# Last head transposes, feed-forward input sums and the last down product, reordered in a fused attention and feed-forward kernel

## The chip, the cores and the metric

The kernel runs on one core of one Trainium2 chip. The metric is the device time of one execution, in microseconds (us). Before the change it was 1168.09 us, the median of three runs (1167.99 to 1169.35). PE is the tensor engine (matmuls), PEld its weight loads, DVE the vector engine, ACT the scalar engine, POOL GpSimd, SP the sync engine. SP and ACT issue the DMA transfers. In the traces, DMA queue q1 carries what SP issues and q10 what ACT issues. L267 is line 267 of the kernel in question. Line numbers shift by a few between versions, so L905 of before is L909 of after, and L977 is L974 in one experiment.

## The reference

Cut to what matters: one transformer block, adaptive layernorm, 32 query heads over 512 keys, then a gated feed-forward network.

```python
# x: (1, 2048, 1024); 32 query heads, 4 key/value heads of 128; F = 3584; all bf16
sa, ca, ga, sb, cb, gb = six rows of silu(c) @ w_mod
h = layernorm(x) * (1 + ca) + sa
q = h @ wq                        # per head 128 columns
p = softmax(q @ k.T * 128**-0.5)  # the last 512 keys of the cache
x = x + ga * (concat_heads(p @ v) @ wo)
h = layernorm(x) * (1 + cb) + sb
x = x + gb * ((silu(h @ w_gate) * (h @ w_up)) @ w_down)
```

## The kernel before

The 2048 rows go through attention in four chunks of 512, 32 heads each. Then comes the chunk's output projection `oproj`. Then two feed-forward stages of 1024 rows each follow, each ending in a "down" product. The large products run as seven smaller ones over sums and differences of blocks (A11, A12, S1, S2, ... on the input side, and the same for the weights), numbered 0 to 6 below. The S sums are made by the vector engine. Weights arrive in "units" of 512 KB, issued by ACT into a few slots.

A head's output is transposed by a DMA on the sync queue, one head late, and four layernorm transposes (`ln_turn`) are issued at head 29, ahead of the last heads:

```python
def oturn(i):
    h = hd(i)
    T.op(tr_queue(), lambda: SP.dma_start_transpose(oT[:, h, :]..., o_sb[i % NOS]),
         reads=[B_os[i % NOS]], writes=B_oT[h])
# in the loop over heads; i counts all heads of all chunks
if ch == NCH - 1 and h == 29:
    ...
    for a_ in kept:
        ln_turn(*a_)
...
pv(i, ...)                      # p @ v of head i, and its division on the vector engine
if i >= 1:
    oturn(i - 1)
```

The output projection goes through its seven products. Between matmuls it calls `each()`, which takes one task from a list that belongs to the coming feed-forward stage. Product 0 loads the chunk's rows of x at its end:

```python
for n in range(len(PRO)):                       # the seven products
    both = n < 4
    for part in range(1 if both else 2):
        for ws in ((0, 1), (2, 3)):             # units of four head pairs
            for k in (0, 1) if both else (part,):
                for w_ in ws:
                    for p in range(NPU * w_, NPU * w_ + NPU):
                        o_mm(n, k, p)
                    each()
            ...
            if n or ws[0]:
                while free:
                    u = free.pop(0)
                    if u < UPC:                 # product 0: behind the last head's transpose
                        load_unit(ch, u, 1, B_oT[hd(Hq - 1)] if n == 0 else ())
            if n == 0 and ws[0]:
                for t in range(TPC):
                    load_x(ch * TPC + t)
        ...
    if n == 0:
        sums(2)                                 # the S2 sums, for product 2
```

The task list is one queue: eight layernorm scalings, then eight "stretch sums", then loads and pair sums at fixed positions. `load_raw` loads gate and up weights:

```python
todo = [lambda kc=kc: ln_scale(1, kc, ...) for kc in range(DT)] + stretch_todo()
rest = [lambda m=m, k=k: sums_of_pair(0, m, k) for m in range(2) for k in range(4)]
at = {18: lambda: load_raw(0), 24: ..., 28: lambda: load_raw(1), 46: lambda: load_raw(2)}
at.update((36 + j, f_) for j, f_ in enumerate(rest))
```

At the end of the kernel each 128x512 tile of the last down product is evicted by `take_product`: add the sum kept in `u_`, multiply by the gate, add to the rows. Then the 256 KB of whole rows are stored.

```python
V.tensor_tensor(u_[0], bank(b), u_[0], ALU.add)
V.tensor_tensor(rt[s_], u_[0], gate[:, lo:lo + CH], ALU.mult)
V.tensor_tensor(x_[:, lo:lo + CH], x_[:, lo:lo + CH], rt[s_], ALU.add)
```

The softmax here doesn't subtract the row's maximum and nothing guards it: scores larger than these inputs give would overflow.

## Time and profile before

| | before |
|---|---|
| median, range | 1168.09 us (1167.99 to 1169.35), 3 runs |
| span of the profiled run | 1165.9 us, clock 1.0 |
| PE, DVE, ACT busy | 98%, 67%, 45% |
| last output projection | about 605.9 to 653.8 us |
| end of the last matmul (its start, 1161.28, plus 0.216), end of the last vector work, last store landed | 1161.5, 1163.57, 1165.61 us |

The lines themselves are in the prediction below. PE is busy nearly all the time, so read the profile for the few places where PE waits and for the tail after its last matmul.

One warning on the column of idle time. The profile models the end of a matmul, 0.38 us after its start, while such matmuls follow one another every 0.216 us. A wait of 1.0 us therefore shows as only about 0.8. In this trace 118 matmul records are missing as well: it has 7789, and the trace of e4 below, a kernel with the same matmuls, has 7907. A missing record leaves 2 x 0.216 - 0.38 = 0.05 us of seeming idle time, so as an estimate some 6 of the 13.4 us of PE's idle time were never idle. Below, a "loss" is counted from start to start: the distance between two matmul starts, less what the first takes at full rate.

### The profile page before, as it was taken

What the parts mean: (1) busy time and instruction counts of PE and PEld (TensorE: products, weight loads), DVE (VectorE), ACT (ScalarE), POOL (GpSimd) and SP (SyncE); (2) the same over time, 40 slices, a digit from 0 to 9 for tenths busy, and PEclk for the clock granted to TensorE, in tenths of its full rate; (3) what the DMA queues carried; (4) which work ended last, traced back from release to release, by engine and by line L of the source; (5) the groups of instructions that cost most, each with busy time, mean ns of one, the idle gap of its engine ahead of it and who ended that gap; (6) DMA issues with size and microseconds to landing.
All of it is one profiled execution on the core that took longest, in us unless ns stands there. A gap on an engine that the chain in (4) does not pass through costs nothing.

```text
span 1165.9 us, 20810 instructions
## 1 busy us (share of the span) xinstructions
PE 1146.7 (98%) x7789; PEld 669.7 (57%) x7907; DVE 786.7 (67%) x1718; ACT 526.2 (45%) x844; POOL 21.7 (2%) x41
## 2 busy tenths in 40 slices
PE   8999999999999999999999999999999999999998
PEld 5787645777548876468864444444444444444443
DVE  4888646877638877347847688888377777776214
ACT  3777503777217775057751244444110344444110
POOL 1000000000000000000000000000010000000000
PEclk9999999999999999999999999999999999999999
DMA  9999796999859997869949765666895232322733
GB/s 289 246 250 260 203 357 231 262 272 257 268 202 284 272 218 210 306 149 287 272 99 349 247 176 182 206 180 175 276 246 179 86 86 77 105 73 65 261 126 135
DMA packets 283876, 245.57 MB, mean 211 GB/s; under 512 B 109952, under 2 KB 247168, under 8 KB 283776
## 3 DMA queue, kind: packets, MB, share of 16 engines
q1 hardware_dynamic: 253328, 179.74, 58.3%
q10 hardware_dynamic: 30448, 64.50, 15.6%
q8 instruction: 63, 1.03, 0.4%
q14 instruction: 37, 0.30, 0.1%
HBM read 189.27 MB, written 30.41 MB: 188 GB/s over the span
## 4 chain that ended last, share of the span: by engine, by line
PE 95%; DMA 2%; DVE 1%; ACT 1%; issue 1%; POOL 0%; DVEq 0%; ACTq 0%
PE ps L267 95%; DMA arena<-in_A_wo_dram 1%; ACT arena L758 1%; DMA arena<-arena 0%; PE ps L271 0%; DVE arena L775 0%; ACT arena L1025 0%; DMA arena<-in_c_dram 0%; ACT arena L742 0%; DVE arena L977 0%; DVE arena L492 0%; DVE arena L372 0%; DVE arena L707 0%; DVE arena L774 0%; DVE arena L980 0%
## 5 line engine op out<-in xcount | busy, mean ns | idle before, releaser
L267 PE MATMUL ps<-arena 128*128 128x512 bf16 (+5 forms) x7740 | 1144.3, 308 | 13.4 <-DVE arena L500 1.2
L267 PEld LDWEIGHTS ps<-arena 128*128 128x128 bf16 (+1 forms) x7858 | 666.9, 98 | 488.4 <-issue 6.8
L758 ACT ACTIVATE arena<-ps 128x1024 bf16<-128x1024 f32 x256 | 262.0, 1027 | 37.6 <-PE ps L267 34.8
L644 DVE TENSOR_TENSOR arena<-arena 128x512 f16<-128x512 bf16 (+3 forms) x510 | 223.1, 481 | 26.5 <-DMA wo_sums<-arena 13.5
L703 ACT ACTIVATE arena<-ps 128x256 f32<-128x256 f32 x180 | 68.7, 382 | 136.7 <-PE ps L267 136.2
L1304 DVE TENSOR_TENSOR arena<-ps,arena 128x512 f16<-128x512 f32 x112 | 77.3, 690 | 40.0 <-PE ps L267 37.9
L1297 ACT ACTIVATE arena<-ps 128x512 f32<-128x512 f32 x112 | 66.9, 597 | 73.6 <-PE ps L267 73.6
L707 DVE TENSOR_TENSOR arena<-ps,arena 128x256 bf16<-128x256 f32 x180 | 75.8, 421 | 32.6 <-PE ps L267 30.4
L775 DVE TENSOR_TENSOR arena<-ps,arena 128x512 bf16<-128x512 f32 x128 | 88.5, 692 | 4.5
L1326 ACT ACTIVATE ps<-ps 128x512 f32<-128x512 f32 x56 | 32.6, 582 | 119.7 <-PE ps L267 119.4
L977 DVE TENSOR_TENSOR arena<-ps,arena 128x512 f32<-128x512 f32 x34 | 23.4, 689 | 87.7 <-PE ps L267 87.6
L774 DVE RECIPROCAL arena<-ps 128x4 f32<-128x4 f32 x128 | 23.2, 181 | 52.5 <-PE ps L267 52.4
L1316 DVE TENSOR_TENSOR arena<-ps,arena 128x512 bf16<-128x512 f32 x56 | 38.6, 688 | 29.7 <-ACT arena L1311 29.7
L1311 ACT ACTIVATE arena<-ps 128x512 f16<-128x512 f32 x56 | 33.3, 595 | 31.6 <-PE ps L267 31.6
L980 DVE TENSOR_TENSOR arena<-ps,arena 128x512 bf16<-128x512 f32 x22 | 15.2, 689 | 46.0 <-PE ps L267 46.0
L428 DVE BATCH_NORM_STATS2 arena<-arena 128x6 f32<-128x512 bf16 x56 | 38.4, 687 | 9.1 <-DMA arena<-x_mid 8.8
L1008 DVE SCALAR_TENSOR_TENSOR arena<-arena 128x512 f32<-128x512 bf16 x56 | 41.6, 743 | 0.1
L1311 ACT ACTIVATE arena<-arena 128x512 f16<-128x512 f16 x56 | 34.8, 622 | 4.9 <-DVE arena L1304 4.9
L379 POOL TENSOR_TENSOR arena<-arena 128x1 f32<-128x1 f32 x30 | 19.2, 641 | 849.1 <-DVE arena L377 849.1
L929 ACT ACTIVATE arena<-ps 128x512 f32<-128x512 f32 x12 | 6.8, 596 | 60.8 <-PE ps L267 60.8
L905 DVE TENSOR_TENSOR arena<-arena 128x1024 f16<-128x1024 bf16 (+1 forms) x48 | 29.7, 686 | 6.2 <-DMA arena<-arena 6.2
L1316 DVE TENSOR_TENSOR arena<-arena 128x512 bf16<-128x512 f16 x56 | 23.8, 425 | 5.0
(61 smaller groups left out, 200.7 us busy)
## 6 DMA issues: line engine op xcount, KB each, us to landing
arena<-wo_sums ACTq DMA_DIRECT2D x46, 512.0 KB, 8.7
arena<-in_A_wq_dram SPq DMA_DIRECT2D x42, 512.0 KB, 4.9
arena<-wq_sums SPq DMA_DIRECT2D x22, 768.0 KB, 6.7
arena<-in_B_w_gate_dram SPq DMA_DIRECT2D x28, 512.0 KB, 4.2
arena<-in_B_w_up_dram SPq DMA_DIRECT2D x28, 512.0 KB, 5.4
arena<-wd_sums ACTq DMA_DIRECT2D x16, 896.0 KB, 6.6
arena<-in_A_wo_dram SPq DMA_DIRECT2D x24, 512.0 KB, 6.5
arena<-in_B_w_down_dram ACTq DMA_DIRECT2D x12, 896.0 KB, 7.4
```

The lines of the kernel that those rows point to most:

```text
L267: T.op(PE, lambda: TE.matmul(out_ap, lhsT, rhs, start=start, stop=stop, skip_group_check=loose), reads=reads, writes=bb)
L428: T.op(DVE, lambda: V.bn_stats(st_sb[i][:, 6 * hf:6 * hf + 6], x_[:, 512 * hf:512 * hf + 512]), reads=[bx], writes=[B_st[i]])
L644: T.op(st, lambda: e.tensor_tensor(dst, x, y, op), reads=reads, writes=[dst_b])
L703: T.op(ACT, lambda: A.activation(sn[k], bank(QBK, 256), AF.Copy), writes=PB[QBK] + [B_sn[k]])
L707: T.op(DVE, lambda: V.tensor_tensor(dst, bank(XBK, 256, off), sn[k], ALU.add), reads=[B_sn[k]], writes=PB[XBK] + [B_q[i % NQ]])
L758: T.op(ACT, lambda: A.activation(ex[i % NEX][:, kt:kt + 2, :], bank(SCB[kt], 1024).rearrange("p (a b) -> p a b", a=2), AF.Exp, scale=att_s ...
L775: T.op(DVE, lambda: V.tensor_tensor(o_sb[i % NOS].rearrange("p (a b) -> p a b", a=TPC), num, rl_bc, ALU.mult), reads=[B_rl], writes=both + ...
L1008: T.op(DVE, lambda: V.scalar_tensor_tensor(acc, ms[:, kc, :], sc[:, kc:kc + 1], acc, op0=ALU.mult, op1=ALU.add), reads=[B_ms, B_sc, B_acc] ...
L1297: T.op(ACT, lambda: A.activation(fn[m][i], bank(b), AF.Copy), writes=PB[b] + [B_fn[m][i]])
L1304: T.op(DVE, lambda: V.tensor_tensor(ring[c_], bank(b), fn[m][i], ALU.add), reads=[B_fn[m][i]], writes=PB[b] + [bs[c_]])
L1311: T.op(ACT, lambda: A.activation(sl_[c_], src, AF.Silu), reads=reads, writes=writes + [B_sl[c_]])
L1316: T.op(DVE, lambda: V.tensor_tensor(dst, u_[0], s_[0], ALU.mult), reads=[s_[1]] + [x for x in u_[1:]], writes=[db] + list(bb))
```

## The change

Its intent is to take away PE's waits in the last output projection, and to shorten the vector work and the store behind the last matmul. It has four parts.

```diff
 # 1. the last four heads are transposed at once; product 0 takes both tiles pair by pair
+            def turned(i):
+                return i >= NA - 4
...
-                        for ws in ((0, 1), (2, 3)):
-                            for k in (0, 1) if both else (part,):
+                        for ws in ((0, 1), (2, 3)) if n else ((0, 1), (2,), (3,)):
+                            if n == 0 and ws[0]:
+                                for p in range(NPU * ws[0], NPU * ws[-1] + NPU):
+                                    o_mm(n, 0, p)
+                                    o_mm(n, 1, p)
+                            for k in ((0, 1) if both else (part,)) if n or not ws[0] else ():
...
-                if i >= 1:
+                if i >= 1 and not turned(i - 1):
                     oturn(i - 1)
+                if turned(i):
+                    oturn(i)
 # 2. the tasks are bound to a product
+            first = {1: [... ln_scale ...],
+                     2: [None] * 5 + [lambda: load_raw(0), ...],
+                     3: stretch_todo(), 4: rest, 5: [None] * 6 + [lambda: load_raw(2)]}
+            first[4].insert(2, lambda: load_raw(1))
 # 3. the rows of x are loaded at head 26 instead of after product 0
-                            if n == 0 and ws[0]:
-                                for t in range(TPC):
-                                    load_x(ch * TPC + t)
+                if ch and h == Hq - 6:
+                    for t in range(TPC):
+                        load_x(ch * TPC + t)
 # 4. the last down product: rows prepared ahead, two operations a tile, last tile in halves
+                        for k in range(4):
+                            ... u2[k] = u2[k] * gate;  u2[k] = u2[k] + x_
+                        ... the same for the part already in bank cb[3], second half
+                        for k in range(4):
+                            ... store the second half of the rows now
+                            for lo, w in ((0, CH),) if k < 3 else ((0, half_), (half_, half_)):
+                                ... matmuls, then u1 = bank * gate; x_ = u1 + u2
+                                ... store these columns on a queue of their own
```

More of the change, by code (lines that the diff above doesn't have):

```diff
@@ L947, in oproj @@
                                         o_mm(n, k, p)
-                                    each()
+                                    each(n)
                             if both or part:
                                 free.extend(n * PPU + w_ + NUN for w_ in ws)
-                            if n or ws[0]:
+                            if n or ws[0] == 3:
                                 while free:
@@ L1211, in _ @@
                 if h == Hq - 1:
-                    oturn(i)
+                    if not turned(i):
+                        oturn(i)
                     if ch == 0:
@@ L1224, in _ @@
                     else:
-                        oproj(ch, (), lambda: None)
+                        oproj(ch, (), lambda n: None)
             NST, NPR, TPS = 2, FT // 2, 2 * TPC
@@ L1387, in stretch_todo, with each @@
                 return [lambda k=k, j=j: stretch_sums(k, j) for k in range(4) for j in range(2)]
-            todo = [lambda kc=kc: ln_scale(1, kc, g2, B_g2, sb, B_sb) for kc in range(DT)] + stretch_todo()
             rest = [lambda m=m, k=k: sums_of_pair(0, m, k) for m in range(2) for k in range(4)]
-            at = {18: lambda: load_raw(0),
-                  24: lambda: T.op(ACT, lambda: A.activation(shift, shift, AF.Silu), reads=B_shift, writes=B_shift),
-                  28: lambda: load_raw(1), 46: lambda: load_raw(2)}
-            at.update((36 + j, f_) for j, f_ in enumerate(rest))
-            todo += [at.pop(j, lambda: None) for j in range(len(todo), 47)]
-            def each():
-                if todo:
-                    todo.pop(0)()
+            todo = []
+            first = {1: [lambda kc=kc: ln_scale(1, kc, g2, B_g2, sb, B_sb) for kc in range(DT)],
+                     2: [None] * 5 + [lambda: load_raw(0),
+                         lambda: T.op(ACT, lambda: A.activation(shift, shift, AF.Silu), reads=B_shift, writes=B_shift)],
+                     3: stretch_todo(), 4: rest, 5: [None] * 6 + [lambda: load_raw(2)]}
+            first[4].insert(2, lambda: load_raw(1))
+            def each(n):
+                for _ in range(1 + (len(first.get(n, ())) > 8)):
+                    if first.get(n):
+                        f_ = first[n].pop(0)
+                        if f_:
+                            f_()
             oproj(NCH - 1, o_done, each)
-            while todo:
-                todo.pop(0)()
+            assert not any(first.values())
             def take_small():
@@ L1494, in _ @@
             Q_xr = [dq("q_xr%d" % i) for i in range(4)]
+            Q_end = [dq("q_end%d" % i) for i in range(5)]
             xr = {}
@@ L1503, in down @@
                 u2 = [None] * 4
+                last = st == NST - 1
                 for k in range(4):
@@ L1519, in down @@
                     w_ = n % NWD
+                    if last and n == len(PROD) - 1:
+                        for k in range(4):
+                            x_, bx = xr[4 + k]
+                            T.op(DVE, lambda: V.tensor_tensor(u2[k], u2[k], gb_bc[:, 0:CH], ALU.mult), reads=[B_gb[0]], writes=[B_u2[k]])
+                            T.op(DVE, lambda: V.tensor_tensor(u2[k], u2[k], x_[:, 0:CH], ALU.add), reads=[bx], writes=[B_u2[k]])
+                        half_ = CH // 2
+                        T.op(DVE, lambda: V.tensor_tensor(u1[3][:, half_:], bank(cb[3], half_, half_), gb_bc[:, half_:CH], ALU.mult),
+                             reads=[B_gb[0]], writes=PB[cb[3]] + [B_u1[3]])
+                        T.op(DVE, lambda: V.tensor_tensor(u2[3][:, half_:], u2[3][:, half_:], u1[3][:, half_:], ALU.add),
+                             reads=[B_u1[3]], writes=[B_u2[3]])
+                        for k in range(4):
+                            t = t0 + 4 + k
+                            x_, bx = xr[4 + k]
+                            B_xe = [_Buf("xe%d" % i) for i in range(2)]
+                            for b_ in B_xe:
+                                b_.absorb(bx)
+                            T.op(Q_out[k], lambda: SP.dma_start(of[t * P:(t + 1) * P, CH:D], x_[:, CH:D]), reads=[bx])
+                            for lo, w in ((0, CH),) if k < 3 else ((0, half_), (half_, half_)):
+                                b = ab[0] if lo else cb[k]
+                                for p in range(NPR):
+                                    mm(bank(b, w, lo), pt[a_][:, p, k * P:(k + 1) * P], wd[n % NWD][:, p, lo:lo + w], lo > 0 and p == 0, p == NPR - 1,
+                                       [B_pt[a_][p], B_wd[n % NWD][p // 7]], PB[b], loose=True)
+                                T.op(DVE, lambda: V.tensor_tensor(u1[k][:, lo:lo + w], bank(b, w, lo), gb_bc[:, lo:lo + w], ALU.mult),
+                                     reads=[B_gb[0]], writes=PB[b] + [B_u1[k]])
+                                T.op(DVE, lambda: V.tensor_tensor(x_[:, lo:lo + w], u1[k][:, lo:lo + w], u2[k][:, lo:lo + w], ALU.add),
+                                     reads=[B_u1[k], B_u2[k]], writes=[B_xe[lo > 0]])
+                                T.op(Q_end[k + (lo > 0)], lambda: SP.dma_start(of[t * P:(t + 1) * P, lo:lo + w], x_[:, lo:lo + w]),
+                                     reads=[B_xe[lo > 0]])
+                        continue
@@ L1566, in _ @@
                 order = [order[i] for i in (6, 7, 2, 3, 0, 4, 1, 5)]
-            for q_ in Q_out:
+            for q_ in Q_out + Q_end:
                 T.wait_all(q_)
```

## The prediction

> **What bounds the kernel now.** I read the page first, then the tensor engine's waits in the stretch the change edits, then the chain of waits there, the DMA view of the same stretch, and the timeline of the last microseconds. The page (line, engine, tiles, count, busy time and mean, idle time before and its releaser):
>
> ```profile
> span 1165.9 us, 20810 instructions
> PE 1146.7 (98%) x7789; PEld 669.7 (57%) x7907; DVE 786.7 (67%) x1718; ACT 526.2 (45%) x844; POOL 21.7 (2%) x41
> PE 95%; DMA 2%; DVE 1%; ACT 1%; issue 1%; POOL 0%; DVEq 0%; ACTq 0%
> L267 PE MATMUL ps<-arena 128*128 128x512 bf16 (+5 forms) x7740 | 1144.3, 308 | 13.4 <-DVE arena L500 1.2
> ```
>
> The tensor engine (PE) is the bound, at full clock, and the change takes no matmul away. It can only win back PE's idle time, 13.4 us in all, or shorten the tail after the last matmul. The change edits two places: the output projection of the last chunk (from 605.9 us to about 653.8 us) and the last down product. PE's waits between 604 and 660 us:
>
> ```profile
> PE ps L267 <- DMA arena<-arena: 1.1, 2, 0.9
> PE ps L267 <- DVE arena L977: 0.8, 1, 0.8
> PE ps L267 <- DMA arena<-in_A_wo_dram: 0.3, 1, 0.3
> PE ps L267 <- DVE arena L775: 0.2, 1, 0.2
> ```
>
> The first is a DMA transpose of a head's output, the second a PSUM eviction behind other vector work, the third a weight unit of the output projection. These figures count idle time after a modelled 0.38 us end of each matmul; start to start a 512-wide matmul takes 0.216 us, so the real losses are larger. Start to start I find: 0.33 and 1.07 us for two transposes (607.2, 607.7), 0.17 us for an input sum (617.7), 0.93 and 0.05 us for the eviction (624.8, 627.4), 0.41 us for the weight unit (642.2). Sum **2.97 us**. The 0.39 us at 604.6 is not touched.
>
> The chain of waits there (start, duration, what) shows that the last of them is more than its 0.3 us:
>
> ```profile
> 625.69 3.70 PE ps L267 x16
> ...
> 629.47 12.97 DMA arena<-in_A_wo_dram
> 642.44 0.14 issue
> 642.58 11.38 PE ps L267 x52
> ```
>
> That unit is issued when its slot is free, and lands 12.97 us later, because its queue is full. So PE and the DMA queue run neck and neck here.
>
> The tail, vector engine's timeline (start, duration):
>
> ```profile
> 1161.70 0.69 DVE L977 TENSOR_TENSOR arena<-ps,arena 128x512 f32<-128x512 f32 x1 [1.14 <-PE ps L267]
> 1162.42 0.69 DVE L980 TENSOR_TENSOR arena<-arena 128x512 bf16<-128x512 f32 x1
> 1163.15 0.42 DVE L981 TENSOR_TENSOR arena<-arena 128x512 bf16<-128x512 bf16 x1
> ```
>
> PE ends at 1161.7, three dependent operations end at 1163.57, and the store (2.0 us from issue to landing, in the issues list) ends the span.
>
> **What the Trainium skill says.** "DMA: Bandwidth & Descriptors", section "Queues, rings and completion order": each DMA engine round-robins between the queue rows that have work, a packet at a time. The trace agrees to the packet. From 622 to 630 us, and from 632 to 640 us (queue, packets, MB, share):
>
> ```profile
> q10 hardware_dynamic: 750, 2.73, 87.1%
> q1 hardware_dynamic: 750, 0.38, 16.8%
> ```
> ```profile
> q10 hardware_dynamic: 1735, 1.74, 70.4%
> q1 hardware_dynamic: 1736, 0.88, 41.4%
> ```
>
> One packet of q1 (the gate and up weights) passes for each one of q10 (the units), and the engines' time is used up. "VectorE: DVE Perf Modes", section "The TRN2 errata": a matmul costs 6+FD cycles at 2.4 GHz, so 216 ns for 512 columns and 109 for 256; the trace has 216 ns, and halving a tile costs PE nothing but 14 x 2 ns. The same section: an fp32 tensor_tensor takes (N+151)/0.96 ns, 691 for 512 and 424 for 256; the trace has 689, and 421 for its 256-wide PSUM additions. "DMA: Bandwidth & Descriptors", section "Anatomy of one DMA": about 2 us of a DMA are fixed, so quartering the last store saves little; the trace's 2.0 us for 256 KB agrees.
>
> **Part 1, heads turned at once, product 0 in another order.** Before, the sync queue issues four layernorm transposes (599.56 to 604.93), then the four last heads at 605.02, 606.34, 607.64 and 608.95, landing 2.4 us later each. Product 0 stands still for the first two (607.48, 608.76). After, only head NA-4 overtakes the layernorm transposes; its output is ready at 599.58. The count of transposes ahead of head NA-3 stays five in all, so it still lands at about 608.8. But the new order does both tiles of heads pair by pair: 12 matmuls from 605.89 need no new head, two more need NA-4, so the first that needs NA-3 comes at 605.89 + 14 x 0.216 = 608.91, just after 608.8. Gain 0.33 + 1.07, with 0.1 us in hand. Product 0 then ends near 609.3.
>
> **Part 2, sums held back.** Before, eight layernorm scalings (8 x 0.33 = 2.6 us) stood ahead of the S2 sums (four of 0.69 us), and eight stretch sums (5.5 us) ahead of product 1's eviction at 624.95. After, S2 begins at 614.5, when the S3 sums end, and its first tile is ready at 615.2, before product 2 at 616.3; then the scalings until 619.8, then the evictions at 619.8 and 621.6, before product 3 at 623.2. The stretch sums come in product 3, which has no eviction on the vector engine, and the pair sums in product 4, on which nothing waits until the feed-forward stage. Gain 0.17 + 0.93 + 0.05. Sum of parts 1 and 2: 2.56 us, with which PE asks for the last unit of product 5 near 639.6 instead of 642.2.
>
> **Part 3, x loaded six heads early: the unit queue decides.** The units can't start before the last head's turn lands (611.38, unchanged). They are 14 loads to the one PE waits for, ten of 128 packets of 4 KB and four of 512 packets of 1 KB, and the DMA engines are 90 to 100% busy. Taking the rows of x (1 MB) out helps only by what they took from the units. Between 613 and 621 us q1 sent 489 packets in 23.6% of 8 us, 1.9 us, most of them x. The gate weights, small packets, will follow at once, since nothing on the sync queue holds them: 489 x (16.8% of 8 us / 750) = 0.9 us. So about 1.0 us is saved, and some 0.2 us more since the gate weights start 2 us earlier, at 610.3, and send part of their packets before the units run. The last unit lands at about 642.4 - 1.2 = 641.2 and not at 639.6. Hence I expect PE to gain **1.2 us** of the 2.97 us in this stage (used at 641.35 against 642.58); the rest becomes a longer wait for the same unit. Moving x in the two middle chunks gains nothing: no DMA wait stands there.
>
> **Part 4, the last down product.** Added ahead of it on the vector engine: four times a product and a sum (0.725 + 0.61 us start to start, from the 0.69 us rows) and two halves of 0.42: 6.1 us from 1150.8 to 1156.9. Before, the first tile was evicted at 1152.63, so it starts 4.3 us behind, but a tile now costs two operations, 1.34 us, against PE's 3.02: tiles end at 1158.3, 1159.6, 1161.0, the first half of the last at 1161.8, where the second half becomes ready. The bank of tile 3 is read by 1156.9, before PE needs it at 1158.7. After the last matmul: 0.42 + 0.03 + 0.42 = 0.87 against 1.87 us, so 1.0 us; the store shrinks from 256 to 64 KB, I take 0.2 us. **1.2 us.**
>
> **Sum:** 1168.09 - 1.2 - 1.2 = **1165.7 us**.
>
> **Rivals.** (a) The units keep pace: all 2.97 us come home, 1163.9 us. For it: x is out of the way, and the 1 KB packets would go faster if the gate and up weights ran out. Against it: those are 4096 packets (2 MB), and one-for-one sharing uses them up only near the last unit. (b) The gate weights simply take x's place: no gain at all in this stage, 1166.9 us. For it: the first units landed only after 7 us even though x was half done by 614. Against: small packets take a third of the time. (c) The vector engine falls behind in the last product, or tile 3's bank is late: plus up to 1 us at the end. Against it: 1.8 us in hand at the bank. (d) Head NA-3's transpose is late: 0.1 to 0.5 us lost again, but under part 3 this vanishes behind the unit anyway.
>
> **Range and chances.** I give the unit queue 60%, (a) 20%, (b) 20%; the tail is 0.9 to 1.4 us. With run scatter of about 0.7 us (1167.99 to 1169.35) I take 1163.6 to 1167.4. The whole stake is 0.3% of the time, so 2% either way is all but excluded: faster 0.005, same 0.99, slower 0.005.
>
> **What would show it.** Right: PE's wait for the transposes and for L977 gone between 604 and 660 us, a wait for in_A_wo of over 1 us near 639 to 641, the last tile's vector work 0.87 us. Wrong: no such wait (rival a), a later landing than 641.8 (b), or a vector engine still busy with tile 2 when PE ends (c).

## The result

After the change the median is **1165.45 us** (1165.27 to 1167.72, four runs), beside 1168.59 us (1167.99 to 1169.35, four runs) for the kernel before on the same chip. The ratio is 0.9977, with a 95% interval of 0.996 to 0.9995. That is the same within 2%, and the predicted 1165.7 us is 0.25 us from the median. All four runs of after had the full clock. A ratio here and below is the mean time of one kernel's fast runs over that of the other's of the same rounds, so it is not quite the ratio of the medians.

The page of after, in the lines that answer those of before (the span; busy time, share and instructions by engine; PE's largest group, with busy time, mean, idle time before it):

```profile
span 1163.5 us, 20969 instructions
...
PE 1153.1 (99%) x7921; PEld 671.3 (58%) x7921; DVE 790.9 (68%) x1726; ACT 526.3 (45%) x844; POOL 21.7 (2%) x41
...
L267 PE MATMUL ps<-arena 128*128 128x512 bf16 (+5 forms) x7872 | 1151.0, 308 | 6.4 <-DVE arena L500 1.2
```

The idle time seems to fall from 13.4 to 6.4 us, while the span falls by 2.4. Most of that fall is the 118 records which the trace of before lacks (after has all of its 7921, 14 of them from the halved tile). Compare losses, not this column.

PE's waits between 604 and 660 us (engine and line, what it waited for: total, times, longest):

```profile
PE ps L267 <- DVE arena L909: 0.7, 1, 0.7
PE ps L267 <- DMA arena<-wo_sums: 0.3, 1, 0.3
PE ps L267 <- DVE arena L775: 0.2, 1, 0.2
```

The waits for the heads' transposes, for the eviction at L977 and for the last weight unit are gone. L775 is the untouched one. Two waits are new. Start to start they are 0.82 us at 616.7 us, for an S2 sum (L909), and 0.44 us at 634.0 us, for a unit of product 4. The losses of the stage went from 2.97 to 1.25 us, a gain of 1.7 us.

The chain of waits of after in the same stretch (start, duration, what) shows where the new ones come from:

```profile
607.67 1.81 DVE arena L909 x3
...
609.66 4.19 DMA arena<-arena
...
616.99 0.69 DVE arena L909
...
621.44 13.12 DMA arena<-wo_sums
...
634.60 21.54 PE ps L267 x99
```

The transpose of the last head took 4.19 us from issue to landing (609.66 to 613.85). Before, it took 2.4 us (608.95 to 611.38). The vector engine's sums wait for it, and so do the weight units on ACT.

The vector engine's timeline at the end of after:

```profile
1160.69 0.42 DVE L1558 TENSOR_TENSOR arena<-ps,arena 128x256 f32<-128x256 f32 x1
1161.15 0.42 DVE L1560 TENSOR_TENSOR arena<-arena 128x256 bf16<-128x256 f32 x1
```

The last store was issued at 1161.60 and landed at 1163.16 us: 1.56 us for 64 KB, against 2.01 us (1163.60 to 1165.61) for 256 KB before.

**A measure with less chance in it.** The time at which attention ends varies from execution to execution. The division (L775) of the last head but one began at 604.15 us in the profiled run of before and at 604.82 us in that of after. Two experiments (e1, e3), whose program up to there is that of before, both had 604.84, and after, run once more (e5), had 604.90. So I measure the *stretch* from that operation's start to the end of the last vector operation. Only the last store lies outside it.

```text
stretch before  1163.57 - 604.15 = 559.42 us
stretch after   1161.57 - 604.82 = 556.75 us    difference -2.67
last store      1.56 - 2.01                                -0.45
sum                                                        -3.12
medians         1165.45 - 1168.59                          -3.14
```

The account closes: 1.7 us in the stage, 1.0 us of vector work in the tail, 0.45 us of store. That it does so to 0.02 us is luck. The interval of the ratio is about 4 us wide, and e1 below shows that the loss at the last unit, which is part of the 1.7 us, scatters by about 1 us from one execution to the next. The spans of the two profiled runs differ by only 2.4 us because attention ended 0.67 us later in that of after.

### The profile page after: what moved, and what is told of

Read it like the earlier page. It is cut to its first block, busy times and chain, and to the rows that moved or that the text cites. A ratio compares the mean times of both kernels' runs of the same rounds, so it can differ in the third digit from the quotient of the medians.

```text
span 1163.5 us, 20969 instructions
## 1 busy us (share of the span) xinstructions
PE 1153.1 (99%) x7921; PEld 671.3 (58%) x7921; DVE 790.9 (68%) x1726; ACT 526.3 (45%) x844; POOL 21.7 (2%) x41
## 4 chain that ended last, share of the span: by engine, by line
PE 94%; DMA 2%; SPq 1%; DVE 1%; ACT 1%; issue 0%; DVEq 0%; ACTq 0%
PE ps L267 94%; DMA arena<-wo_sums 1%; DMA arena<-in_w_mod_dram 1%; ACT arena L758 0%; DVE arena L909 0%; SPq L295 0%; DMA arena<-arena 0%; SPq L288 0%; SPq L310 0%; DVE arena L775 0%; ACT arena L1030 0%; SPq L277 0%; ACT arena L742 0%; DVE arena L707 0%; SPq L321 0%
## 5 line engine op out<-in xcount | busy, mean ns | idle before, releaser
L644 DVE TENSOR_TENSOR arena<-arena 128x512 f16<-128x512 bf16 (+3 forms) x510 | 223.0, 480 | 27.8 <-DMA wo_sums<-arena 18.9
L775 DVE TENSOR_TENSOR arena<-ps,arena 128x512 bf16<-128x512 f32 x128 | 88.5, 691 | 4.5
L982 DVE TENSOR_TENSOR arena<-ps,arena 128x512 f32<-128x512 f32 x30 | 20.7, 688 | 76.8 <-PE ps L267 75.4
L909 DVE TENSOR_TENSOR arena<-arena 128x1024 f16<-128x1024 bf16 (+1 forms) x48 | 29.6, 684 | 9.1 <-DMA arena<-arena 9.1
```

Source lines behind the costliest of these rows:

```text
L644: T.op(st, lambda: e.tensor_tensor(dst, x, y, op), reads=reads, writes=[dst_b])
L775: T.op(DVE, lambda: V.tensor_tensor(o_sb[i % NOS].rearrange("p (a b) -> p a b", a=TPC), num, rl_bc, ALU.mult), reads=[B_rl], writes=both + ...
```

## The experiments

Theory A: PE's waits in the stage are one coupled system with the DMA queue of the weight units. Parts 1 and 2 take waits away, but PE then only arrives earlier at units that aren't there. The early load of x (part 3) makes their gain real. Rival B: the parts are worth what each removes, and x early is worth only its own megabyte. A second question came from the trace of after: why does the last head's transpose take 4.2 us? "Stretch" is the measure above; a kernel with the old tail stands 0.98 us higher in it than the same kernel with the new one. All outputs were correct, since only order and timing were edited.

| kernel | median us (range) | before beside it | ratio (95%) | stretch | against before |
|---|---|---|---|---|---|
| before | | | | 559.42 | |
| after | 1165.45 (1165.27-1167.72) | 1168.59 | 0.9977 (0.996-0.9995) | 556.75 | -2.67 |
| e1_tail | 1167.6 (1167.29-1169.74) | 1168.7 | 0.9992 (0.9979-1.0006) | 559.07 | -0.35 |
| e2_turns | 1171.34 (1170.76-1174.38) | 1168.7 | 1.0024 (1.0011-1.0038) | 561.76 | +2.34 |
| e3_sums | 1168.6 (1166.48-1170.46) | 1168.7 | 0.9997 (0.9984-1.001) | 560.32 | +0.90 |
| e4_x_early | 1166.83 (1166.56-1168.31) | 1168.7 | 0.9984 (0.9972-0.9997) | 557.48 | -1.94 |
| e5_after_again | 1165.55 (1165.38-1167.83) | 1169.12 | 0.9976 (0.9964-0.9987) | 556.78 | -2.64 |
| e6_x_late | 1169.94 (1168.49-1174.31) | 1169.12 | 1.0011 (0.9998-1.0025) | 560.38 | +0.96 |
| e7_raw_behind_turn | 1165.8 (1164.43-1167.72) | 1169.12 | 0.9973 (0.996-0.9986) | 556.88 | -2.54 |
| e8_ln_behind | 1189.09 (1186.07-1189.41) | 1169.12 | 1.0165 (1.0151-1.0178) | 580.07 | +20.65 |
| e9_no_turn | 1163.92 (1163.66-1164.87) | 1169.38 | 0.9956 (0.9944-0.9968) | 556.41 | -3.01 |
| e10_ln_first | 1164.66 (1163.43-1167.01) | 1169.38 | 0.9963 (0.9951-0.9976) | 556.32 | -3.10 |
| e11_ln_first_fill | 1163.11 (1162.28-1167.34) | 1169.38 | 0.9954 (0.9941-0.9967) | 555.96 | -3.46 |
| e12_rows_behind | 1163.46 (1163.23-1164.09) | 1168.83 | 0.9953 (0.9939-0.9966) | 555.10 | -4.32 |

### e1_tail: part 4 alone

```diff
 # before, with these of the change and nothing else
+            Q_end = [dq("q_end%d" % i) for i in range(5)]
+                last = st == NST - 1
+                    if last and n == len(PROD) - 1:
+                        ... the whole block of part 4
-            for q_ in Q_out:
+            for q_ in Q_out + Q_end:
```

> The last down product of the change alone, on the kernel before. Theory: the tail after the last matmul stands by itself, 4.2 us before (1161.7 to 1165.9) and 2.8 us in the changed kernel, so about 1.4 us faster than before, ratio near 0.9988, with the waits of the output projection as before. Rival: a half of the gain belongs to the profiled pair only (noise), then under 0.7 us.

The median is 1167.6 beside 1168.7 us. The last matmul ended at 1162.82 and the last vector operation at 1163.91, so 1.09 us apart instead of 2.07; the last store took 1.57 us. So the tail is worth 0.98 + 0.44 = 1.4 us, as in after. The stretch fell by only 0.35 us because in this execution the untouched stage before it lost 1.31 us to the unit which cost 0.41 us in before (about 0.9 us more, with the same instructions there). A wait on the unit queue scatters by that much between executions, so one profile of a kernel that has such a wait is good to about 1 us only; the kernels without it agree much closer (after, e5 and e7 below to 0.13 us).

### e2_turns: part 1 alone

```diff
 # before, with part 1 as shown above (turned, product 0 pair by pair); x stays late:
-                            if n == 0 and ws[0]:
+                            if n == 0 and ws[0] == 3:
                                 for t in range(TPC):
                                     load_x(ch * TPC + t)
```

> The last heads turned at once and product 0 in its new order, alone on the kernel before. Theory (the parts hang together): the 1.4 us of waits for transposes vanish from product 0, but the S2 sums still stand behind the layernorm scalings and end no earlier, so product 2 starts at about the same time and waits some 1.5 us there; net gain 0 to 0.3 us. Rival (the losses simply add): 1.4 us faster.

It is slower: 1171.34 beside 1168.7 us, and the stretch grows by 2.34 us. PE's waits between 604 and 660 us:

```profile
PE ps L267 <- DVE arena L909: 1.9, 1, 1.9
PE ps L267 <- DMA arena<-in_A_wo_dram: 1.7, 2, 1.4
```

That is outside both expectations. The waits for transposes in product 0 are gone, as intended. In their place stand 2.11 us (start to start) for an S2 sum and 0.51 and 1.54 us for weight units, and at 838.9 us 1.16 us for a W_down half. Ahead of that S2 sum stood four of the layernorm scalings (1.38 us), as the theory had it, and the late transpose, which it had not. The last head's transpose landed at 614.6 us, 4.2 us after its issue. It is the same new delay as in after, here without the other parts to soften it.

### e3_sums: part 2 alone

```diff
 # before, with part 2 as shown above and nothing else
-                                    each()
+                                    each(n)
-            todo = [... ln_scale ...] + stretch_todo()
+            first = {1: [... ln_scale ...], 2: [... load_raw(0) ...], 3: stretch_todo(), 4: rest, 5: [... load_raw(2)]}
```

> The feed-forward sums held back, alone on the kernel before. Theory (units decide): the waits for the S2 sums and for the L977 eviction vanish (1.15 us), but the last unit of product 5 still lands near 642.4 and the wait for it grows from 0.4 to about 1.5 us; net gain under 0.4 us. Rival (losses add): 1.15 us faster, no longer wait for a unit.

The median doesn't move (1168.6 beside 1168.7 us), and the stretch is 0.90 us longer. PE's waits between 604 and 660 us:

```profile
PE ps L267 <- DMA arena<-in_A_wo_dram: 2.4, 2, 1.4
PE ps L267 <- DMA arena<-arena: 0.9, 1, 0.9
```

The waits for the S2 sum and the eviction are gone, and PE loses 1.24 and 1.53 us at the units instead. This is the "new wait in place of the old" of Theory A.

### e4_x_early: part 3 alone

```diff
-                            if n == 0 and ws[0]:
-                                for t in range(TPC):
-                                    load_x(ch * TPC + t)
...
+                if ch and h == Hq - 6:
+                    for t in range(TPC):
+                        load_x(ch * TPC + t)
```

> Only the rows of x loaded at head 26, alone on the kernel before. Theory: the units land about 1 us earlier, which takes away the 0.4 us wait for the last one and no more, since product 0, the S2 sums and the eviction still hold PE up: gain 0.2 to 0.5 us. Rival: the gate weights take the place of x and nothing changes, or the first packets of gate weights behind the last turn make it land later (as in the changed kernel, 4.2 us after issue) and it is up to 1 us slower.

The part that sounds least is the only one of the first three which gains alone: 1166.83 beside 1168.7 us, the stretch 1.94 us shorter. The largest line of PE's waits in the stage:

```profile
PE ps L267 <- DVE arena L974: 0.8, 1, 0.8
```

Only the eviction behind other vector work is left of the four waits (plus the untouched L775). The unit that PE waited for at 642.2 us before landed at 639.0 us instead of 642.4. The product-0 waits went too: the last head's transpose landed at 610.6 us although attention ended 0.8 us later than in before. By the losses, product 0 is 1.40 of the 1.98 us that the stage gains here, the unit 0.41 and the S2 sum 0.17, so most of it does not come from the unit queue, and the theory (0.2 to 0.5 us) missed it. In e4 the first layernorm transpose was issued at 598.61 us, 1 us earlier than in before. What let it go earlier was not tested, and it is not reliable: in e9 below, with x early as well, 0.93 us of the loss in product 0 is back.

Counting by the stretch, the four parts alone add up to -0.35 + 2.34 + 0.90 - 1.94 = +0.95 us; together they give -2.67. The medians say the same, though each is good to about 1 us only: alone -1.1, +2.6, -0.1 and -1.9, together -0.4, against -3.1 for the change. Rival B is out, since the parts are not additive; e6 below, where the early x is worth about twice what it is worth here, shows it once more.

### e5_after_again and e6_x_late: the change, with and without x early

e5 is the changed kernel once more, as a control. e6 is the changed kernel with x back after product 0:

```diff
+                            if n == 0 and ws[0] == 3:
+                                for t in range(TPC):
+                                    load_x(ch * TPC + t)
...
-                if ch and h == Hq - 6:
-                    for t in range(TPC):
-                        load_x(ch * TPC + t)
```

> The changed kernel once more, for a second trace and five more rounds. Theory A (the gate weights right behind the last turn hold up its landing): the last transpose lands about 4.2 us after its issue again, the S2 sums are late by about 0.8 us again, and a unit of product 4 is waited for. Theory B (an accident of that one execution): it lands after about 2.4 us and the wait for S2 is gone. The 0.5 us that the first trace lost at 246 us, before any changed instruction, should be gone or elsewhere, as chance would have it. Time near 1165.5 us.

> The changed kernel with the rows of x loaded where they were, after product 0. Theory of the prediction (x delays the units, one packet for one): the last unit that PE waits for lands about 1 us later than without x in the way, so 0.5 to 1.2 us slower than the changed kernel. Rival: x in front keeps the gate weights off the last turn, which then lands in 2.4 us, and the two cancel, within 0.4 us.

e5 repeats the result (1165.55 us) and, to 0.03 us, the stretch. e6 has 1169.94 us in the same rounds: with x late the whole change gains nothing against before (ratio 1.0011). Waits of PE in the stage of e6:

```profile
PE ps L267 <- DMA arena<-in_A_wo_dram: 1.4, 1, 1.4
PE ps L267 <- DVE arena L989: 1.2, 1, 1.2
PE ps L267 <- DMA arena<-wo_sums: 0.6, 1, 0.6
```

The first two are unit waits. The second is put down to L989 because that semaphore came last in the records, but the unit which product 5 needs landed at just that time: 642.2 us for the one and 644.6 us for the other, against 639.1 and 640.6 us in after. So x early is worth 4.4 us in the medians and 560.38 - 556.75 = 3.63 us in the stretch. That is more than the whole change, and far more than the 0.5 to 1.2 us expected.

The reason is in x itself and in the loads behind it on the sync queue. In after, the four gate and up loads issued from 610.9 to 613.8 us landed at 615.3, 617.8, 627.0 and 635.7 us. In e6, x goes first, and the corresponding loads landed at 630.8, 637.8, 642.5 and 650.8 us. The trace of after between 632 and 640 us (queue: packets, MB, share of the DMA engines), which answers the second pair of lines in the prediction:

```profile
q10 hardware_dynamic: 2303, 2.81, 105.3%
q1 hardware_dynamic: 142, 0.07, 3.1%
```

Before, 1736 small packets of q1 passed in this window beside 1735 of q10. Now q1 is done, and the units move 2.81 MB instead of 1.74. A unit lands every 1.5 us instead of every 2.4.

The packets in the traces can be counted by their size: on q1, those of 2 KB are x and those of 512 bytes the gate and up weights. From the issue of the first unit to the landing of the second unit of product 5, all packets together took 31.9 us of the 16 engines' time in e6 and 27.8 us in after. Of the 4.1 us between them, x is 2.3 us, the weights are 1.2 us and the units 0.5 us. So x's own packets are the larger part, and the weights' head start is the smaller.

### e7_raw_behind_turn: why does the last transpose take 4.2 us?

The first suspicion was the gate and up weights, which the change lets start beside the transpose. e7 is after with the first pair of these loads waiting until the last transpose has landed:

```diff
-                     2: [None] * 5 + [lambda: load_raw(0), ...
+                     2: [None] * 5 + [lambda: load_raw(0, [B_oT[hd(Hq - 1)][0]]), ...   # passed on as behind=
```

> The changed kernel with the first gate and up loads waiting for the last turn's landing. Theory A (gate packets on the same ring hold up the last transpose's semaphore): it lands 2.4 us after issue, units start 2 us earlier, the 0.8 us wait for S2 goes; the weights then compete with the units longer, so the last units may be waited for; net 0.3 to 1 us faster than the changed kernel. Theory B (instruction fetch or chance): the landing stays late and the time is the same within 0.3 us.

In the trace the loads went out only at 628.5 us, later than meant, so no weights were on the queue during the transpose. It was issued at 609.9 us and landed at 614.2: 4.3 us, no faster. The S2 wait is still there (0.96 us), so the weights are not the cause. The unit of product 4 is no longer waited for, but at 664.5 us PE loses 0.40 us that after does not lose. The queue is now empty enough to see more. All packets of e7 between 612.2 and 614.5 us:

```profile
DMA packets 3, 0.02 MB, mean 7 GB/s; under 512 B 2, under 2 KB 2, under 8 KB 2
...
q8 instruction: 1, 0.02, 2.6%
q1 hardware_dynamic: 2, 0.00, 0.1%
```

The transpose's data is through by 612.2 us. One 16 KB packet of a queue that the profile calls "instruction" follows; it takes 0.96 us (2.6% of 16 engines' 2.3 us). Then, at 613.2 us, come two 4-byte packets of q1, and only after them does the transpose count as landed. The same window over the last transpose, issue to landing, in before (608.9 to 611.4 us) and in after (609.6 to 613.9 us):

```profile
q1 hardware_dynamic: 1068, 0.26, 50.9%
```
```profile
q1 hardware_dynamic: 1882, 0.67, 64.5%
q8 instruction: 1, 0.02, 1.6%
```

In all five traces with the new head order (after, e2, e5, e6, e7) an instruction packet falls at 611.5 to 612.3 us and the last transpose takes 4.1 to 4.3 us; it lands 1.0 to 1.2 us after that packet's end in each of them. In the traces with the old head order, or with the layernorm transposes moved away (e8 and e10 to e12), it takes 2.4 us. Where I looked up the packet there (before, e1, e4, e9, e10, e11), it falls at 613.4 us or later; in e12 it falls at 612.5 us, also after the landing (610.5). The packet stands in the transpose's way in these records. Which engine's instructions it fetches, and why the new order brings it forward, was not settled, and no experiment here moved that packet by itself.

### e8_ln_behind: the layernorm transposes behind the last heads

This is after with the four layernorm transposes issued after the last head's, so that the heads don't stand in line:

```diff
                 if ch == NCH - 1 and h == 29:
                     ...
-                    for a_ in kept:
-                        ln_turn(*a_)
...
                     if ch == NCH - 1:
+                        for a_ in kept:
+                            ln_turn(*a_)
                         break
```

> The changed kernel with the four layernorm transposes behind the last heads instead of ahead of three of them. Theory (the sync queue's order sets when the last head lands, and so when sums and units start): the last turn lands near 609.5 instead of 611.4 to 613.9, the waits for S2 and for a unit (0.82 and 0.44 us in the changed kernel's trace) vanish, 0.8 to 1.3 us faster than the changed kernel. Rival: the layernorm transposes then collide with the units and the scalings come late, so product 1's eviction holds PE up again: no gain.

The last head's transpose did land at 610.9 us after 2.4 us. But the kernel took 1189.09 us, over 20 us more. PE's two largest waits in the stage, and the vector engine's timeline (idle time before the operation and its releaser in brackets):

```profile
PE ps L267 <- DVE arena L982: 15.4, 1, 15.4
PE ps L267 <- DMA arena<-wo_sums: 4.2, 1, 4.2
```
```profile
643.60 2.67 DVE L392 TENSOR_SCALAR arena<-arena 128x512 bf16<-128x512 bf16 x8 [27.04 <-DMA arena<-arena]
```

The layernorm transposes now run beside the weight units. Issued at 609.8, 611.1, 612.5 and 621.5 us, they landed at 613.1, 625.8, 637.5 and 643.5 us. The vector engine stood before the scalings of the layernorm (L392) for 27 us. The evictions behind them, and with them PE, stood too. A part of the loss is no wait: the granted clock was 0.5 from 624.4 to 631.2 us and from 634.6 to 651.7 us, and 22 matmuls there took some 0.43 us each instead of 0.216, together 4.6 us. The rival came true, and far beyond "no gain". So in this kernel the layernorm transposes belong before the units.

### e9_no_turn: the change without part 1

```diff
-                if i >= 1 and not turned(i - 1):
+                if i >= 1:
                     oturn(i - 1)
-                if turned(i):
-                    oturn(i)
 # and product 0 in its old order
```

> The changed kernel without its first part: heads turned one head late and product 0 in the old order, with x early, the sums held back and the new last product. Theory (in every trace with the new head order the last turn lands 4.2 us after issue, in every one with the old order 2.4 us, so the new order gives back at the S2 sums what it wins in product 0): within 0.5 us of the changed kernel, or up to 1 us faster, since the run with x early alone showed no wait in product 0 either. Rival (part 1 is worth its 1.4 us): 1 to 1.5 us slower than the changed kernel.

It is not slower than the change, so the rival is out: 1163.92 us, ratio 0.9956 beside 0.9976 for e5, from another chip; the two intervals overlap a little. PE's one wait left in the stage besides L775, and the transpose that causes it in the chain of waits (start, duration):

```profile
PE ps L267 <- DMA arena<-arena: 0.8, 1, 0.8
```
```profile
605.45 2.43 DMA arena<-arena
```

PE loses 0.93 us in product 0, start to start. The last head's transpose takes 2.4 us again, the S2 sums are in time, and the units wait for nothing. So part 1 buys 0.93 us in product 0 and pays 0.82 + 0.44 us later: 0.3 us worse than leaving it out, and the stretch agrees (556.41 against 556.75). That is one trace of e9, and product 0 lost nothing in e4, so the sign is likely and the size is not sure. The medians of e9 and of e5 differ by 1.6 us. The trace accounts for 0.34 us of that; in the profiled runs the rest lies before the stretch, which began at 603.74 us in e9 against 604.90 in e5, where the edit touches only the order of two transposes on the sync queue. Whether that is chance or has a cause stays open.

### e10_ln_first and e11_ln_first_fill: heads in front of no one

If the layernorm transposes can't go behind the last heads, they can go ahead of the last five. e10 is after with them issued in head NA-4:

```diff
                 if ch == NCH - 1 and h == 29:
                     ...
-                    for a_ in kept:
-                        ln_turn(*a_)
...
+                if i == NA - 4:
+                    for g_ in list(tasks):
+                        finish(g_)
+                    for a_ in kept:
+                        ln_turn(*a_)
```

e11 adds two matmuls of product 0 into the last head, to cover the L775 wait that no part of the change touches:

```diff
-            o_list = [(k, p) for k in range(2) for p in range(8)]
+            o_list = [(k, p) for k in range(2) for p in range(8)] + [(0, 8), (1, 8)]
-                    for _ in range(4):
+                    for _ in range(4 + 2 * (i == NA - 1)):
```

> The changed kernel with the four layernorm transposes one head earlier, in head NA-4, ahead of all of the last five heads. Theory (the sync queue hands out about 1.3 us per transpose, and what counts is how many stand before the last head): the last head is issued near 607.2 when its data is ready, instead of 609.7, lands near 609.6, the S2 sums are ready before product 2, the units start 4 us earlier and no unit is waited for: about 1.2 us faster than the changed kernel. Rival: the turns of heads NA-5 and NA-4 come later than product 0 wants them, or the instruction packet hits another transpose: no gain.

> The same, with two more matmuls of product 0 (pair 8, both tiles) in the last head, before its value product, where all versions so far lose 0.39 us waiting for a vector operation. Theory: 0.4 us faster than the run with the layernorm transposes first. Rival: the gap only moves to the wait for the last head's own bank or turn, no gain.

In e10 all the losses of the stage are gone but that of L775 (0.39 us). In e11 that one is gone as well: PE does not lose anything from 603 to 660 us. But both lose 0.82 to 0.87 us at a new place, in the first feed-forward stage's down product. This is the one line of PE's waits from 604 us to the end in e11:

```profile
PE ps L267 <- DMA arena<-in_B_w_down_dram: 0.7, 1, 0.7
```

e11 has 1163.11 us, ratio 0.9954, below both kernels. Its profiled run was its slowest (1167.34 us). By the stretch it stands 0.79 us below after in spite of the new wait: 1.25 + 0.39 - 0.87 = 0.77. The two theories had 1.2 us for e10 and 0.4 us more for e11; the stretch gives 0.43 us, because of the new wait, and 0.36 us more.

### e12_rows_behind: the new wait taken away too

The second half of that W_down load lands at 837.6 us in e11. It shares the DMA engines with four rows of x_mid, which are needed later than it. e12 is e11 with these rows issued behind it:

```diff
-                for k in range(4):
-                    xr[k] = load_rows(Q_xr[k], t0 + k, (196, 198, 200, 188)[k], True)
                 for n, (a_, _) in enumerate(PROD):
                     load_wd(n + 1)
+                    if n == 0:
+                        for k in range(4):
+                            xr[k] = load_rows(Q_xr[k], t0 + k, (196, 198, 200, 188)[k], True, behind=[B_wd[1][1]])
```

> The version of e11_ln_first_fill, with the first four rows of x_mid that a down product needs issued only after the second W_down half has landed (the sync queue waits for it), in both down phases. In e11 the tensor engine lost 0.87 us at 836.5 us to the second half of that load, which shared the DMA engines with those rows. Theory (the rows took the load's share): that loss falls to under 0.2 us, and the median comes to 1163.1 - 0.8 = 1162.3 us against 1169.4 before, ratio about 0.9948. Rival 1 (the load is slow because of the wd_sums stores and the layernorm rows, not of these rows): the loss stays at 0.6 us or more, median 1163.1. Rival 2 (the rows now land after the first product's evictions want them): vector waits for x_mid of over 2 us at 838 to 842 us, and the tensor engine may lose some of it at the next bank; median 1163 to 1164.

The loss is gone, so the theory's cause holds, and PE waits for nothing from 604 us to the last matmul. PE's largest group on the page of e12 has 5.1 us of idle time before it, all of it in the start and in attention:

```profile
L267 PE MATMUL ps<-arena 128*128 128x512 bf16 (+5 forms) x7872 | 1151.2, 308 | 5.1 <-DVE arena L500 1.2
```

The stretch falls by 0.86 us, as much as the loss was. The median does not show it: 1163.46 us and ratio 0.9953, beside 1163.11 us and 0.9954 for e11 from another call. Both intervals are about 0.0027 wide, 3 us, so the medians couldn't have shown it, nor the 1162.3 us that the theory expected. e12 is the best kernel by the trace. By the clock it and e11 are alike, and both are faster than before by 0.5%.

## Why the prediction was right

The number was right (1165.7 against 1165.45 us). Not every term under it was, and the wait on which its main case rested did not come. Two errors had opposite signs, and that they left so little is luck.

- **What bounds the kernel:** right. PE was the bound, no matmul went away, and all that was gained came from PE's losses and the tail. But "13.4 us in all" overstated what there was to win, because about half of it is missing records.
- **Part 1, product 0:** the step "it still lands at about 608.8 ... with 0.1 us in hand" held. Product 0 has no loss in after, so rival (d) did not occur. The step that failed is in part 3, "the last head's turn lands (611.38, unchanged)". It landed at 613.85 us, of which 0.7 us is the later end of attention and 1.8 us the longer transpose. e7 shows an instruction packet in that time and rules out the weights. By e9, part 1 as built costs some 0.3 us more than it gains.
- **Part 2, sums held back:** the eviction wait did vanish (0.93 + 0.05 us). The claim that S2 "begins at 614.5" failed with the transpose: a sum that product 2 needs began at 616.99 us, and PE lost 0.82 us where I had booked a gain of 0.17.
- **Part 3, the unit queue:** I gave 60% to a wait of over 1 us for in_A_wo near 639 to 641 us. It was named as the sign of being right, and it did not come. The mechanism, units sharing the DMA engines packet by packet with gate and up weights, is what the traces show. The size was off: I credited x early with 1.0 + 0.2 us, and between e6 and after the unit of product 5 landed 4.0 us earlier (644.6 against 640.6). The mis-sized terms are the 1.9 us for x, the 0.9 us of gate weights that were to "follow at once" in its place, and the "some 0.2 us more". From the first unit's issue to the landing of that unit, x took 3.1 us of the 16 engines' time in before and none in after, and the weights took 6.2 and 5.9 us: they did not move up into x's place. 790 of their 4096 packets had gone out before the first unit, and the rest were used up by 635.7 us, some 5 us before that unit, where I had them used up "only near the last unit". So the units came at full rate at the end. The late transpose had a share in this, since it held the first unit back by 2.5 us (613.87 against 611.40) while the weights ran. Rival (b), which had the weights simply take x's place, is out by the same runs. What was lost instead was 0.44 us for an earlier unit, in product 4. Since part of what the stage loses still stayed lost (1.25 us), this is neither my main case nor rival (a), which had all of it coming home.
- **Sum of the stage:** 1.2 us was predicted and 1.7 us measured. The undersized effect of x and the overlooked delay of the last transpose compensated for the most part, by chance. The 1.7 us is itself good to about 1 us, since before's loss at the last unit scatters.
- **Part 4, the tail:** right in the vector work (1.0 us predicted, 0.98 measured; rival (c) did not occur, PE never waited). The store was taken as 0.2 us and is worth 0.45. The reason given for it in the prediction, a fixed cost that the skill states for DMAs of GpSimd, did not apply to a store from the sync queue and has been cut there.
- **Sum:** 2.4 us was predicted from all parts and 3.1 us measured by stretch and store. The median came out so close to the prediction because I started from 1168.09 us, and the kernel before ran at 1168.59 us in the comparison. That is luck too.

## What to carry to other kernels

Before you remove a wait of the tensor engine, look at what it will ask for next and when that lands. With a full DMA queue behind it, two of the three reorderings here were worth nothing or less alone, and a load moved out of the queue's busy time was worth more than the whole change. Check that an order that saves time at one place doesn't delay something on which two other engines wait. For effects below half a percent, measure from a marker just before the edited place to the end in the trace: where no queue wait scattered, three traces (after, e5, e7) agreed to about 0.1 us, where the medians of five runs leave 3 us open. Where one does, a single trace is good to about 1 us.

## What the Trainium skill lacked or had wrong

- "Runtime: NRT & Kernel Launch", section "Instruction fetch mechanics", says that instructions are fetched by DMA in blocks of 16 KiB and calls the cost mostly hidden. No page says what such a fetch does to a transfer that is under way; that would belong to "DMA: Bandwidth & Descriptors", section "Queues, rings and completion order". In e7 one 16 KB instruction packet took 0.96 us, and the transpose around it took 4.3 us where 2.4 is usual. No experiment moved the packet by itself.
- "DMA: Bandwidth & Descriptors", section "DMA Transpose (X-bar)": the pages have figures for a DMA transpose (the time of one 128x128 tile, an effective bandwidth), but none for a transpose from SBUF to SBUF beside loads. Here a head's transpose took 2.4 us with the queue near empty, and in e8 layernorm transposes beside the weight units took 15, 25 and 22 us (611.1 to 625.8, 612.5 to 637.5, 621.5 to 643.5).
- "DMA: Bandwidth & Descriptors" gives a fit of a fixed cost and a rate for DMAs of GpSimd only, and none for a store from the sync queue. Here a whole store of 64 KB took 1.56 us, against 2.01 us for 256 KB.
